# Fused attention and two expert layers on one core: the subtraction that makes the low halves of the exponentials, in pieces of 576 columns

## The chip, the cores and the metric

One NeuronCore of a Trainium2 chip runs the kernel. The metric is the device time of one execution in microseconds (us), smaller is better. The engines are named as in the profile: PE (TensorE, matrix products), DVE (VectorE), ACT (ScalarE), POOL (GpSimd) and SP (SyncE, which here only starts DMAs).

## What is computed

```python
q_pool = q.reshape(B, H, S // 2, 2, D).mean(axis=3)        # B=2, H=8, S=1152, D=64
scores = q_pool @ k.transpose(0, 1, 3, 2) / np.sqrt(D)
scores = scores - np.max(scores, axis=-1, keepdims=True)
attn = np.exp(scores)
attn = attn / (np.sum(attn, axis=-1, keepdims=True) + 1e-09)
x = attn @ v                                   # 1152 tokens of 512
# moe: every token goes to one of 8 experts (argmax of a cosine score), 512 -> 1024 -> 512, relu
# moe2: out = ((x @ w_a) * (x @ w_b)) @ w_out, inner width 1536
```

## The kernel before

The program has three stages: attention (to about 265 us of the profiled span), the experts (to about 460 us) and the last, dense layer. Attention works on 8 pairs of heads; a pair has 9 units of 128 pooled queries against 1152 keys, so there are 72 units, numbered j. The order of instructions on each engine is written out by hand: `att_step(i)` issues, for step i, the scores of unit i on PE (L374), the row maximum `nm` of unit i on DVE (L379), the exponential of unit i-1 on ACT into a tile `e` of 128x1152 (L384), and for unit i-2 the split of `e` into two half-precision parts. The first part `ehl[:, 0]` is a rounded copy, on ACT (L396); at one or two places in a pair ACT does only the first 768 columns and DVE the other 384 (L398, the CAST rows). The second part `ehl[:, 1]` is `e` minus the first part (`lo16`, L407), on POOL, for units 63 and 67 on DVE. Two units share one `ehl` tile; when both are filled, SP starts one DMA that transposes the four parts into `eT` (L413). PE multiplies `eT` with the values (L461) seven steps after the scores. One unit in each pair but the last (number 6 of 9), and the last three units of all, are transposed on PE instead and have no `lo16`.

Each engine takes its instructions strictly in this order. Beside them DVE and ACT prepare the next pair: `kT` and `qT` (L71, L75, L225, L226) and the two parts of the values, `vh` on ACT (L259) and `vl` on DVE (L262; two of 128x576 in a pair, which read `vs` and `vh` from SBUF). POOL also makes `qd` (L188, three in a pair).

For batch 0 the routing of the tokens (small DVE instructions in a chain) runs beside units 40 and later. Units 48 to 62 (`LO_PARTS`) already have their subtraction in four instructions of 288 columns; all others have one of 1152. The tiles `e` rotate through 3 buffers (L384 waits for the subtraction three units before), `ehl` and `eT` through 3 each.

Of the kernel before, what the change touches and what calls it, by code (L numbers as in the profile page):

```python
# [43 lines left out]
LO_PARTS = range(48, 63)  # L44
# [17 lines left out]
def fused(ctx, tc, q, k, v, emb, tau, w1, w2, wa, wb, wo, out):  # L62
# [337 lines left out]
    def lo16(j):  # L400
        if j not in two_of:
            return
        ehl = U[j]["ehl"]
        eng = nc.vector if j in LO_DVE else nc.gpsimd
        n = 288 if j in LO_PARTS else 1152
        for a in range(0, 1152, n):
            eng.tensor_tensor(out=ehl[:, 1, a:a + n], in0=U[j]["e"][:, a:a + n], in1=ehl[:, 0, a:a + n], op=ALU.subtract)  # L407

# [369 lines left out]
    def att_step(i):  # L778
# [19 lines left out]
        at(rowmax, i)  # L798
        turn("d")
        at(lo16, i - 2)  # L800
        turn("s")
        at(trans, i - 2)
# [555 lines left out]
```

## Time and profile before

| | us |
|---|---|
| three runs of the kernel | 695.67, 695.88, 692.66 (median 695.67) |
| the profiled execution | 693.38 |
| its span | 691.7 |
| PE busy | 618.1 |
| DVE busy | 493.5 |
| ACT busy | 373.6 |
| POOL busy | 322.3 |

The profiled execution took 1.7 us more than its span. In the rows, a time stands as start and duration in us from the start of the span; what stands in brackets is how long the engine had been idle and what ended that. "x2" means that two instructions are told in one row, from the start of the first to the end of the last. [...]

### The profile page before, as it was taken

What the parts mean: (1) busy time and instruction counts of PE and PEld (TensorE: products, weight loads), DVE (VectorE), ACT (ScalarE), POOL (GpSimd) and SP (SyncE); (2) the same over time, 40 slices, a digit from 0 to 9 for tenths busy, and PEclk for the clock granted to TensorE, in tenths of its full rate; (3) what the DMA queues carried; (4) which work ended last, traced back from release to release, by engine and by line L of the source; (5) the groups of instructions that cost most, each with busy time, mean ns of one, the idle gap of its engine ahead of it and who ended that gap; (6) DMA issues with size and microseconds to landing.
All of it is one profiled execution on the core that took longest, in us unless ns stands there. A gap on an engine that the chain in (4) does not pass through costs nothing.

```text
span 691.7 us, 13314 instructions
## 1 busy us (share of the span) xinstructions
PE 618.1 (89%) x5280; PEld 556.1 (80%) x5280; DVE 493.5 (71%) x796; ACT 373.6 (54%) x518; POOL 322.3 (47%) x271
## 2 busy tenths in 40 slices
PE   6688979889878788998989987969999999999996
PEld 5477767778767677998879877859999999999995
DVE  5978989887899977659947697974355575665523
ACT  3868886987665766456545675426243324233210
POOL 3958878785767941433424665673011212112100
PEclk9779999998988899999999998999999999999998
DMA  9979899998987789884898986454012213121012
GB/s 290 269 176 233 200 217 234 213 211 198 196 198 184 180 202 263 279 277 124 292 332 252 366 315 226 124 160 160 1 62 81 101 62 123 61 70 54 0 46 95
DMA packets 203075, 123.27 MB, mean 178 GB/s; under 512 B 149240, under 2 KB 174840, under 8 KB 203008
## 3 DMA queue, kind: packets, MB, share of 16 engines
q1 hardware_dynamic: 201536, 117.65, 62.3%
q0 software_dynamic: 1472, 4.72, 1.9%
q8 instruction: 43, 0.70, 0.4%
q14 instruction: 24, 0.20, 0.1%
HBM read 72.11 MB, written 13.67 MB: 124 GB/s over the span
## 4 chain that ended last, share of the span: by engine, by line
PE 49%; DVE 22%; ACT 4%; DMA 4%; issue 4%; POOL 1%; SPq 1%; DVEq 0%; ACTq 0%
PE ps_s L1165 21%; PE ps_s L890 4%; DVE nm L379 4%; PE ps_o L1187 4%; PE ps_m L1187 3%; PE ps_y L1187 3%; PE ps_o L461 2%; PE ps_s L374 2%; DVE vl L262 2%; DMA w2r<-in_moe_w_dram 2%; PE ps_m L933 2%; DMA eT<-ehl 2%; PE ps_y L933 1%; DVE cvt L1078 1%; DVE cvt L1079 1%
## 5 line engine op out<-in xcount | busy, mean ns | idle before, releaser
L407 POOL TENSOR_TENSOR ehl<-e,ehl 128x288 f16<-128x288 f32 (+1 forms) x99 | 152.3, 1557 | 63.7 <-issue 31.7
L75 POOL TENSOR_TENSOR wl<-cvt,wh 128x512 fp32r<-128x512 f32 x36 | 48.6, 1364 | 150.1 <-ACT wh L71 146.5
L75 POOL TENSOR_TENSOR w2l<-w2r,w2h 128x512 fp32r<-128x512 f32 x42 | 66.1, 1592 | 92.4 <-ACT w2h L71 46.9
L384 ACT ACTIVATE e<-ps_s,nm 128x1152 f32<-128x1152 f32 x72 | 87.8, 1220 | 37.2 <-DVE nm L379 25.1
L379 DVE TENSOR_REDUCE nm<-ps_s 128x1 f32<-128x1152 f32 x72 | 97.2, 1350 | 12.9 <-PE ps_s L374 12.7
L374 PE MATMUL ps_s<-kTh,qT 64*128 64x512 f32 (+2 forms) x480 | 98.2, 398 | 2.3 <-issue 1.2
L461 PEld LDWEIGHTS <-eT 128*128 128x128 f16 x1863 | 74.8, 102 | 16.6 <-issue 5.6
L461 PE MATMUL ps_o<-vh,eT 128*128 128x65 f16 (+1 forms) x1224 | 78.4, 203 | 10.3 <-DMA eT<-ehl 3.1
L374 PEld LDWEIGHTS ps_s<-kTh,qT 64*128 64x128 f32 x480 | 74.2, 206 | 8.5 <-issue 2.4
L461 PE MATMUL ps_o<-vl,eT 128*128 128x65 f16 (+1 forms) x612 | 73.2, 203 | 0.0
L1175 DVE TENSOR_TENSOR asb<-ps_s,asb 128x384 f32<-128x384 f32 x36 | 20.0, 554 | 69.1 <-PE ps_s L1165 69.1
L396 ACT ACTIVATE ehl<-e 128x1152 f16<-128x1152 f32 (+1 forms) x62 | 69.1, 1114 | 0.0
L71 ACT ACTIVATE abh<-asb 128x384 fp32r<-128x384 f32 x36 | 18.9, 525 | 84.3 <-DVE asb L1175 84.3
L374 PE MATMUL ps_s<-kTl,qT 64*128 64x512 f32 (+2 forms) x240 | 47.9, 367 | 1.5 <-DVE kTl L75 1.5
L1170 ACT ACTIVATE asb<-ps_s 128x384 f32<-128x384 f32 x36 | 17.7, 492 | 57.5 <-PE ps_s L1165 57.2
L374 PEld LDWEIGHTS ps_s<-kTl,qT 64*128 64x128 f32 x240 | 44.3, 209 | 2.1 <-DVE kTl L75 2.1
L75 DVE TENSOR_TENSOR w1l<-w1r,w1h 128x1024 fp32r<-128x1024 f32 x32 | 41.0, 1280 | 4.4 <-ACT w1h L71 3.6
L890 PE MATMUL ps_s<-xhi,w1l 128*128 128x256 f32 x128 | 38.0, 297 | 4.0 <-DVE w1l L75 4.0
L890 PE MATMUL ps_s<-xhi,w1h 128*128 128x256 f32 x128 | 38.4, 300 | 0.0
L75 DVE TENSOR_TENSOR abl<-asb,abh 128x384 fp32r<-128x384 f32 x36 | 20.7, 574 | 24.5 <-ACT abh L71 24.5
L890 PE MATMUL ps_s<-xlo,w1h 128*128 128x256 f32 x128 | 37.7, 294 | 0.0
L71 ACT ACTIVATE w1h<-w1r 128x1024 fp32r<-128x1024 f32 x32 | 34.0, 1063 | 0.0
(277 smaller groups left out, 1743.5 us busy)
## 6 DMA issues: line engine op xcount, KB each, us to landing
w1r<-in_moe_w_dram SPq DMA_DIRECT2D x32, 512.0 KB, 5.6
w2r<-in_moe_w_dram SPq DMA_DIRECT2D x32, 512.0 KB, 5.9
raw<-in_moe_w_a_dram SPq DMA_DIRECT2D x6, 1024.0 KB, 5.4
raw<-in_moe_w_b_dram SPq DMA_DIRECT2D x6, 1024.0 KB, 6.2
raw<-in_moe_w_out_dram SPq DMA_DIRECT2D x6, 1024.0 KB, 5.1
vs<-in_v_dram SPq DMA_DIRECT2D x8, 576.0 KB, 5.1
qs<-in_q_dram SPq DMA_DIRECT2D x16, 256.0 KB, 4.2
ks<-in_k_dram SPq DMA_DIRECT2D x7, 576.0 KB, 5.9
```

The source lines that it names most:

```text
L71: nc.scalar.activation(out=dst, in_=src, func=AF.Copy)
L75: (engine or nc.vector).tensor_tensor(out=dst, in0=src, in1=hi.bitcast(F32), op=ALU.subtract)
L374: nc.tensor.matmul(ps[:, c:c + n], qT[x][r:r + 64, o:o + 128], kT[y][r:r + 64, h, k0:k0 + n], start=i == 0, stop=i == len(ops) - 1)
L379: nc.vector.tensor_reduce(out=nm, in_=U[j]["ps"][:, 256:1408], axis=AX.X, op=ALU.max, negate=True)
L384: nc.scalar.activation(out=e, in_=U[j]["ps"][:, 256:1408], func=AF.Exp, bias=U[j]["nm"])
L396: nc.scalar.activation(out=ehl[:, 0, :c], in_=U[j]["e"][:, :c], func=AF.Copy)
L407: eng.tensor_tensor(out=ehl[:, 1, a:a + n], in0=U[j]["e"][:, a:a + n], in1=ehl[:, 0, a:a + n], op=ALU.subtract)
L461: nc.tensor.matmul(o, eT[:, 9 * x + n, :], v_[:, KEYS[n], :], start=(n == 0 and x == 0 and v_ is vh), stop=(n == 8 and x == 1))
L890: nc.tensor.matmul(p[:, 256 * j:256 * j + 256], a[:, kk, P * j:P * j + P], x[:, kk, :], start=(kk == 0 and x is xhi and a is w1h), stop=(k ...
L933: nc.tensor.matmul(y, a[:, j, P * t:P * t + P], w[:, j, :], start=(c == 0 and j == 0 and a is hh and w is w2h), stop=(c == 3 and j == 1 an ...
L1165: nc.tensor.matmul(p[:, :384], w[:, kk, :], y[:, kk, :], start=(kk == 0 and x == 0), stop=(kk == 3 and x == 2))
L1187: nc.tensor.matmul(F[n]["o"][t], a[:, P * t:P * t + P], w, start=(j == 0 and x == 0), stop=(j == 1 and x == 2))
```

## The change

```diff
         ehl = U[j]["ehl"]
         eng = nc.vector if j in LO_DVE else nc.gpsimd
-        n = 288 if j in LO_PARTS else 1152
+        n = 288 if j in LO_PARTS else 576
         for a in range(0, 1152, n):
             eng.tensor_tensor(out=ehl[:, 1, a:a + n], in0=U[j]["e"][:, a:a + n], in1=ehl[:, 0, a:a + n], op=ALU.subtract)
```

47 subtractions on POOL and 2 on DVE (units 63 and 67) become two instructions each. The same elements are read and written.

On POOL, in the third pair, the rows before (each row one instruction: its line, what it writes and reads, its size, and the engines and DMA queues whose semaphores it waits for):

```order
L407 TENSOR_TENSOR ehl<-e,ehl 128x1152 [waits Activation_49]
L188 TENSOR_TENSOR qd<-qs 128x384 [waits DMAHW1_49,DMAHW0_49]
L407 TENSOR_TENSOR ehl<-e,ehl 128x1152 [waits DMAHW2_49,Activation_49,Pool_49]
L407 TENSOR_TENSOR ehl<-e,ehl 128x1152 [waits DVE_49,Activation_49]
L407 TENSOR_TENSOR ehl<-e,ehl 128x1152 [waits DMAHW4_49,Activation_49,Pool_49]
L256 MEMSET vh 128x9 [waits PE_49]
```

And the same place now:

```order
L407 TENSOR_TENSOR ehl<-e,ehl 128x576 [waits Activation_49]
L407 TENSOR_TENSOR ehl<-e,ehl 128x576
L188 TENSOR_TENSOR qd<-qs 128x384 [waits DMAHW1_49,DMAHW0_49]
L407 TENSOR_TENSOR ehl<-e,ehl 128x576 [waits DMAHW2_49,Activation_49,Pool_49]
L407 TENSOR_TENSOR ehl<-e,ehl 128x576
L407 TENSOR_TENSOR ehl<-e,ehl 128x576 [waits Activation_49]
L407 TENSOR_TENSOR ehl<-e,ehl 128x576 [waits DVE_49]
L407 TENSOR_TENSOR ehl<-e,ehl 128x576 [waits DMAHW4_49,Activation_49,Pool_49]
L407 TENSOR_TENSOR ehl<-e,ehl 128x576
L256 MEMSET vh 128x9 [waits PE_49]
```

The second half of a unit waits for nothing, except in the units whose last 384 columns DVE has cast, where the wait for DVE has moved to the second half.

On ACT, in the fourth pair, before (e and ps_s are the exponentials and the scores):

```order
L384 ACTIVATE e<-ps_s_1531,nm 128x1152 [waits DVE_49,Pool_49]
L396 ACTIVATE ehl<-e 128x1152 [waits DMAHW0_49,Activation_49]
L71 ACTIVATE kTh<-ps_m 128x512 [waits PE_49]
L384 ACTIVATE e<-ps_s_1589,nm 128x1152 [waits DVE_49,Pool_49]
L396 ACTIVATE ehl<-e 128x1152 [waits Activation_49]
```

And now:

```order
L384 ACTIVATE e<-ps_s_1553,nm 128x1152 [waits DVE_49,Activation_49,Pool_49]
L396 ACTIVATE ehl<-e 128x1152 [waits DMAHW0_49,Activation_49]
L71 ACTIVATE kTh<-ps_m 128x512 [waits PE_49]
L384 ACTIVATE e<-ps_s_1611,nm 128x1152 [waits DVE_49,Pool_49]
L396 ACTIVATE ehl<-e 128x1152 [waits Activation_49]
```

36 of the 72 exponentials have a further wait, for ACT itself; the DMAs that transpose have a wait for ACT added in the same way. No instruction but the subtractions has another place in its row.

## Rows read from the trace of the kernel before

**Rows 1.** The page: span, and busy time of each engine.

```profile
span 691.7 us, 13314 instructions
PE 618.1 (89%) x5280; PEld 556.1 (80%) x5280; DVE 493.5 (71%) x796; ACT 373.6 (54%) x518; POOL 322.3 (47%) x271
```

**Rows 2.** Stretches: length, busy us (instructions) by engine, PEclk, DMA share, GB/s.

```profile
62.00:92.00 30.00, 26.39 (x403) 22.63 (x401) 27.40 (x49) 25.91 (x31) 24.30 (x14) 1.00 0.94 218
121.00:151.00 30.00, 26.95 (x406) 23.37 (x407) 27.57 (x50) 26.32 (x33) 23.68 (x14) 1.00 1.07 210
460.00:691.70 231.70, 225.54 (x1196) 210.88 (x1195) 119.37 (x177) 74.41 (x123) 42.60 (x35) 0.99 0.22 73
```

**Rows 3.** POOL's subtractions of 1152: busy us, mean ns, idle before them.

```profile
L407 POOL TENSOR_TENSOR ehl<-e,ehl 128x1152 f16<-128x1152 f32 x47 | 114.5, 2439 | 51.3 <-issue 22.1 <-ACT ehl L396 14.0 <-PE ps_m L204 11.6
```

**Rows 4.** Timeline of POOL: start us, duration us, instruction.

```profile
25.16 7.67 POOL L407 TENSOR_TENSOR ehl<-e,ehl 128x1152 f16<-128x1152 f32 x3
...
42.15 2.38 POOL L407 TENSOR_TENSOR ehl<-e,ehl 128x1152 f16<-128x1152 f32 x1 [6.47 <-PE ps_m L204]
...
76.42 5.22 POOL L407 TENSOR_TENSOR ehl<-e,ehl 128x1152 f16<-128x1152 f32 x2
...
85.87 2.38 POOL L407 TENSOR_TENSOR ehl<-e,ehl 128x1152 f16<-128x1152 f32 x1
...
188.64 2.81 POOL L407 TENSOR_TENSOR ehl<-e,ehl 128x288 f16<-128x288 f32 x4
```

**Rows 5.** Timeline of DVE: the values' second part, the casts, one subtraction.

```profile
29.29 4.17 DVE L262 SCALAR_TENSOR_TENSOR vl<-vs,vsc,vh 128x576 f16<-128x576 f32 x2
...
42.49 2.66 DVE L262 SCALAR_TENSOR_TENSOR vl<-vs,vsc,vh 128x576 f16<-128x576 f32 x1
...
51.05 1.45 DVE L262 SCALAR_TENSOR_TENSOR vl<-vs,vsc,vh 128x576 f16<-128x576 f32 x1
...
59.56 0.90 DVE L398 CAST ehl<-e 128x384 f16<-128x384 f32 x1
...
72.43 0.81 DVE L262 SCALAR_TENSOR_TENSOR vl<-vs,vsc,vh 128x576 f16<-128x576 f32 x1
...
77.81 1.59 DVE L262 SCALAR_TENSOR_TENSOR vl<-vs,vsc,vh 128x576 f16<-128x576 f32 x1
...
86.47 2.00 DVE L398 CAST ehl<-e 128x384 f16<-128x384 f32 x1
...
101.41 2.28 DVE L262 SCALAR_TENSOR_TENSOR vl<-vs,vsc,vh 128x576 f16<-128x576 f32 x1
...
171.27 2.38 DVE L262 SCALAR_TENSOR_TENSOR vl<-vs,vsc,vh 128x576 f16<-128x576 f32 x1
...
192.24 0.72 DVE L653 TENSOR_TENSOR oh<-L,rmx 128x40 f32<-128x40 f32 x1
...
245.80 1.35 DVE L407 TENSOR_TENSOR ehl<-e,ehl 128x1152 f16<-128x1152 f32 x1
...
255.54 0.35 DVE L398 CAST ehl<-e 128x384 f16<-128x384 f32 x1
```

**Rows 6.** Timeline at 234 us: POOL's twelve quarters, and DVE.

```profile
234.10 8.91 POOL L407 TENSOR_TENSOR ehl<-e,ehl 128x288 f16<-128x288 f32 x12
...
235.02 4.67 DVE L262 SCALAR_TENSOR_TENSOR vl<-vs,vsc,vh 128x576 f16<-128x576 f32 x1
```

**Rows 7.** PE after a stop: timeline, then the stretch behind it.

```profile
45.80 0.56 PE L424 MATMUL ps_m<-ident,e 128*128 128x128 f32 x3 [2.14 <-DVE kTl L75]
...
45.80:48.00 2.20, 2.20 (x32) 2.10 (x34) 1.80 (x3) 1.38 (x2) 2.20 (x2) 0.59 0.01 5
```

**Rows 8.** The chain of waits at a transposing DMA: start us, us, what.

```profile
143.63 10.69 DMA eT<-ehl
```

**Rows 9.** ACT's waits ahead of the exponentials: duration ns, min/median/max.

```profile
L384 ACTq EVENT_SEMAPHORE  x62: 17/17/38, 20.7 to 265.7; - x62
```

## Prediction

> **What bounds the kernel now.** I read the page first, then a table of stretches, then the timelines of POOL and DVE side by side, last the chain of waits. PE is busy for 618.1 of 691.7 us [rows 1], but that is an average: in the last 231.7 us it is busy for 225.5 with POOL at 42.6 [rows 2], and nothing that the change touches runs there. The edited instructions lie between 18 and 263 us, in attention. There no engine is full: in the stretches 62 to 92 and 121 to 151 us, which hold about one pair each, DVE is busy for 27.40 and 27.57 of 30.00 us, PE for 26.39 and 26.95, ACT for 25.91 and 26.32, POOL for 24.30 and 23.68, and the DMA share is 0.94 and 1.07 [rows 2]. DVE is the fullest, PE stands 0.6 to 1.0 us behind it. So a microsecond saved on DVE is not wholly a microsecond of the end.
>
> Part of DVE's busy time is waiting. `vl` alone takes 0.81 us (at 72.43), but 2.66 at 42.49, 2.28 at 101.41 and 2.38 at 171.27; the cast alone takes 0.35 (255.54), but 2.00 at 86.47 [rows 5]. In each case a subtraction of POOL was running: one ran from 42.15 for 2.38, to 44.53 [rows 4], and `vl` ended at 45.15, so that its own 0.81 began at 44.34, 0.19 before POOL's end. Either DVE starts about when POOL ends, or it doesn't wait at all. The small routing instructions behind quarters of 288 columns wait less: 0.72 at 192.24 [rows 5].
>
> **The change, part by part.**
>
> *What POOL pays.* Four quarters took 2.81 us where one piece takes 2.38 [rows 4]: three more starts cost 0.43, so one costs 0.14. Two halves then take 2.52, and the 47 units cost 6.6 us of POOL. Most of that lies in POOL's idle time, 51.3 us ahead of these instructions [rows 3]. The cover is gone where units stand one behind the other: the chain goes through a transposing DMA at 143.63, for 10.69 us [rows 8], which starts as soon as the fourth unit of such a run is done; 4 x 0.14 = 0.56 us later now. There is one more such run, a pair of pairs earlier. Between 0 and 1.1 us for both; I take 0.6, the middle, since half of the time PE has other work until the DMA lands.
>
> *What DVE gets.* If DVE comes in behind the first half, that is at 1.26 - 0.19 = 1.07 us after POOL's start in place of 2.38 - 0.19 = 2.19, it wins 1.12 us wherever it arrives within the first 1.07 us. At 42.49 it arrives 0.34 after POOL, at 86.47 0.60 after 85.87 [rows 4, 5]. There are six such places: `vl` at 42.49, 101.41 and 171.27, the second `vl` of the row at 29.29, behind the third of the units from 25.16, and two casts of 2.00, of which one stands in the rows. 6 x 1.12 = 6.7 us. At eight others DVE arrives in the second half, as at 77.81, which is 1.39 after 76.42 [rows 4, 5] and the earliest of them; they wait 0.14 longer, 1.1 us. Net 5.6 us less on DVE. By the table of stretches [rows 2] PE is late next, 0.6 to 1.0 us behind DVE in each pair, and ACT just behind it; with in-order queues less than that comes through. I take half, 2.8 us, and keep 0 and 5.6 as ends.
>
> [...]
>
> *What ACT pays.* 36 exponentials get a third wait, each an own entry in ACT's row. They are long fulfilled, and such an entry takes 17 ns [rows 9]: 0.6 us, half of it on the path, 0.3. The DMAs' added wait costs as little, and only the two on the chain count.
>
> *What DVE pays.* Units 63 and 67 have two starts. Two pieces of 576 columns are at most 2 x 0.81 = 1.62, against 1.35 in one [rows 5]: 0 to 0.27 each; I take 0.1 for both, since the 0.81 belongs to a heavier instruction.
>
> *Does the port come free between two halves?* This is the term on which the sign rests, and no row shows halves. For it: at 192.24 the small instruction waited about 0.5 us behind a quarter within a unit and then ran, as some twenty others of the routing do, and two casts; and between whole units DVE always got in, as at 77.81, in the middle of two units that stand back to back. Against it: at 235.02 `vl` took 4.67 us while POOL ran twelve quarters without a pause from 234.10 [rows 6]. Their pace is 0.69 us, so five or six of them went past the waiting `vl`. One loss among over twenty; I take it that DVE gets in. [...]
>
> *Sum.* -2.8 (DVE) - 1.0 (PE's clock) + 0.6 (transposes) + 0.3 (ACT) + 0.1 (DVE's starts) = -2.8 us. Against the profiled execution's 693.38 that gives 690.6. This execution lies 2.3 below the median of the runs shown, 695.67; on the median the forecast is 695.67 - 2.8 = **692.9 us**, 0.4% faster. A measurement of this kernel can tell about 0.5%, 3.5 us, from no change, so this counts as no change.
>
> **The rivals.**
>
> 1. *All of it comes through.* DVE sets the pace of attention, its 5.6 us are saved whole, and PE keeps its clock at the three places: -5.6 - 2.9 + 1.0 = -7.5, so 688.2. For it: DVE's 91% and `vl` on the chain; at 42.49 both the wait and PE's slow stretch lie ahead of the same next row maximum. Against it: PE and ACT within 1.7 us of DVE, and a DMA share about 1 [rows 2], which a shorter attention doesn't lighten.
>
> 2. *DVE doesn't come in, and nothing else happens.* Every one of the fourteen waits is 0.14 longer, 2.0 us, half of it on the path, 1.0; with the transposes' whole 1.1 and ACT's and DVE's 0.4 it is +2.5, so 698.2: no change either.
>
> 3. *DVE starves where units stand back to back.* As at 235.02 it also misses the gap between two units, which are now a row of halves, and waits for a whole further unit, 2.5 us. The places are the units from 25.16, those at 76.42 and the two that stand the same way a pair of pairs later: 3 x 2.5 = 7.5, half on the path 3.8, on top of rival 2: +6.3, so 702.0. It decides (more than 3.5 us slower) from the first such place on: 2.5 + 1.25 = 3.75. For it: the row at 235.02. Against it: these three places have whole pieces now, and DVE gets in at all three.
>
> That the change doesn't do what it says is excluded by the order of instructions; only DVE could be elsewhere, since every shift of 0.3 us moves an arrival from one half to the other (77.81 misses the first half by 0.32).
>
> **How the numbers follow.** The forecast with half of the gain 0.48, a quarter of that (0.12) beyond 3.5 us faster; rival 1 0.24; rival 2 0.12; rival 3 0.12; shifts that put POOL's lateness on more of the transposes 0.04. Faster 0.12 + 0.24 = 0.36, same 0.36 + 0.12 = 0.48, slower 0.12 + 0.04 = 0.16. The range: from rival 1, 688.2, with 0.7 for the scatter of the runs, 687.5, to a little over rival 2, 699.0, which leaves out most of rival 3 and the rest.
>
> **What would show it.** In the new profile no `vl` or cast before 182 us should be over 1.9 us (0.81 + 1.07), and the six places should be 1.0 to 1.1 shorter; POOL's L407 should be busy about 6 to 7 us more. If the three slow stretches of PE are gone and attention ends by 7 us earlier, rival 1 holds. If a `vl` of over 2.4 us stays, DVE doesn't get in between halves; if one is over 3, rival 3. If POOL's halves end later than 2.6 us after their start with no DVE instruction between them, a start costs more than 0.14. The forecast is wrong if the DMA waits of PE grow by more than 3 us, or if the stretch behind 265 us, which I take as shifted whole, changes its length.

## The result, and the profile after

The changed kernel takes 684.14 us (median of 20 runs, 678.55 to 687.96), the kernel before 691.98 in as many runs beside it (687.15 to 695.88). The ratio is 0.9897, 95% interval 0.9875 to 0.9919: **about 7.1 us or 1.0% faster**. The forecast was 692.9 with a range from 687.5, and no change as the likeliest case, so it was wrong: the time lies below its range. Two things are in the miss of 8.8 us. 3.7 of it is the base: I put the sum on the median of three runs, 695.67, and over 20 runs the kernel before takes 691.98 (from that base the range would have begun at 683.8). The rest, 4 to 5 us, is the sum itself: -2.8 in place of -7.1. One execution of the experiments, of the kernel without the conflict and in halves, ran in a slower state of the chip, and its ratio and median leave it out.

The page of the changed kernel, span and busy time of each engine (to be set beside [rows 1]):

```profile
span 683.4 us, 13368 instructions
PE 612.4 (90%) x5280; PEld 550.5 (81%) x5280; DVE 484.0 (71%) x798; ACT 373.2 (55%) x518; POOL 328.4 (48%) x318
```

DVE has lost 9.5 us, POOL has gained 6.1. POOL's subtractions in halves in the changed kernel, grouped by shape (busy us, mean ns, idle before them), where [rows 3] had 47 of 1152 columns in 114.5 us:

```profile
L407 POOL TENSOR_TENSOR ehl<-e,ehl 128x576 f16<-128x576 f32 x94 | 124.6, 1349 | 35.6 <-issue 25.7 <-ACT ehl L396 8.5 <-POOL qd L188 0.9
```

The timeline of POOL in the changed kernel (start us, duration us), the same places as in [rows 4]:

```profile
25.71 8.52 POOL L407 TENSOR_TENSOR ehl<-e,ehl 128x576 f16<-128x576 f32 x6
...
41.80 3.04 POOL L407 TENSOR_TENSOR ehl<-e,ehl 128x576 f16<-128x576 f32 x2 [5.02 <-issue]
...
52.23 2.52 POOL L407 TENSOR_TENSOR ehl<-e,ehl 128x576 f16<-128x576 f32 x2
...
225.73 8.95 POOL L407 TENSOR_TENSOR ehl<-e,ehl 128x288 f16<-128x288 f32 x12
```

And the timeline of DVE in the changed kernel, which answers to [rows 5] and, with its last three rows, to [rows 6] and what follows there:

```profile
29.60 3.49 DVE L262 SCALAR_TENSOR_TENSOR vl<-vs,vsc,vh 128x576 f16<-128x576 f32 x2
...
41.88 1.82 DVE L262 SCALAR_TENSOR_TENSOR vl<-vs,vsc,vh 128x576 f16<-128x576 f32 x1
48.11 0.81 DVE L262 SCALAR_TENSOR_TENSOR vl<-vs,vsc,vh 128x576 f16<-128x576 f32 x1
...
86.13 0.92 DVE L398 CAST ehl<-e 128x384 f16<-128x384 f32 x1
100.17 1.05 DVE L262 SCALAR_TENSOR_TENSOR vl<-vs,vsc,vh 128x576 f16<-128x576 f32 x1
105.63 0.81 DVE L262 SCALAR_TENSOR_TENSOR vl<-vs,vsc,vh 128x576 f16<-128x576 f32 x1
...
192.79 1.35 DVE L262 SCALAR_TENSOR_TENSOR vl<-vs,vsc,vh 128x576 f16<-128x576 f32 x1
...
226.63 3.31 DVE L262 SCALAR_TENSOR_TENSOR vl<-vs,vsc,vh 128x576 f16<-128x576 f32 x1
234.35 1.61 DVE L407 TENSOR_TENSOR ehl<-e,ehl 128x576 f16<-128x576 f32 x2
235.88 0.81 DVE L262 SCALAR_TENSOR_TENSOR vl<-vs,vsc,vh 128x576 f16<-128x576 f32 x1
```

At 41.88 `vl` arrives 0.08 after POOL's start and ends at 43.70, so its own 0.81 began at 42.89, 1.09 after POOL's start: behind the first half. In turn the second half came later: the three pairs of halves with a `vl` in between took 3.04, 3.05 and 3.04 (from 41.80, 99.32 and 165.70), an undisturbed one 2.52. No `vl` or cast ahead of 182 us is over 1.83 now; before, the longest took 2.92 (the second `vl` of the row at 29.29) and 2.66.

How far each place has moved shows where the gain is made. The `vl` at 200.30, the first for the pair of heads numbered 6, is at 192.79 (-7.5). The `vl` at 235.02 is at 226.63 (-8.4), and its successor has come from 247.06 to 235.88 (-11.2). Of these further 2.8 us, 1.4 are the shorter wait of this `vl` (3.31 in place of 4.67), beside subtractions that the change leaves as they were; where the other 1.4 come from isn't separated. The first expert matmul (L890) has come from 271.1 to 261.7 (-9.4) and the end of the span from 691.7 to 683.4 (-8.3). So nearly all is made in the first 190 us; some more at 226 to 236, and most of that is given back behind it.

What is waited for there stands in the chain of waits. In the changed kernel, from 246 us (start, duration, what the chain went through):

```profile
249.87 2.53 POOL ehl L407 x2
252.40 4.32 SPq L413
...
256.89 4.64 SPq L413
...
263.50 5.54 DMA xr<-xbuf
269.04 0.14 issue
269.18 0.63 PE ps_t L838 x4
```

The same stretch in the kernel before goes through DVE:

```profile
235.10 4.58 DVE vl L262
...
245.80 1.35 DVE ehl L407
247.15 0.73 DVE vl L262
...
257.87 1.80 DVE ehl L407
```

Once DVE is early, the chain goes through POOL's last subtractions, the transposes behind them in SP's queue, and the read of `xr`, the tokens of the second group of expert matmuls, that is queued behind those; PE stands still for it for 2.02 us ahead of 269.18.

### The profile page after: what moved, and what is told of

Its sections match the earlier page's. It is cut to its first block, busy times and chain, and to the rows that moved or that the text cites. A ratio compares the mean times of both kernels' runs of the same rounds, so it can differ in the third digit from the quotient of the medians.

```text
span 683.4 us, 13368 instructions
## 1 busy us (share of the span) xinstructions
PE 612.4 (90%) x5280; PEld 550.5 (81%) x5280; DVE 484.0 (71%) x798; ACT 373.2 (55%) x518; POOL 328.4 (48%) x318
## 3 DMA queue, kind: packets, MB, share of 16 engines
q0 software_dynamic: 1472, 4.72, 2.0%
## 4 chain that ended last, share of the span: by engine, by line
PE 43%; DVE 7%; DMA 4%; issue 3%; SPq 3%; POOL 2%; ACT 1%; DVEq 0%; ACTq 0%
PE ps_s L1165 21%; PE ps_s L890 4%; PE ps_o L1187 4%; PE ps_m L1187 4%; PE ps_y L1187 4%; DMA w2r<-in_moe_w_dram 2%; PE ps_m L933 1%; PE ps_o L933 1%; PE ps_y L933 1%; SPq L413 1%; DVE cvt L1079 1%; PE ps_s L895 1%; DVE cvt L1078 1%; DVE w1l L75 1%; DMA ybuf<-ys 1%
## 5 line engine op out<-in xcount | busy, mean ns | idle before, releaser
L407 POOL TENSOR_TENSOR ehl<-e,ehl 128x576 f16<-128x576 f32 (+1 forms) x146 | 162.0, 1137 | 45.5 <-issue 34.3
L384 ACT ACTIVATE e<-ps_s,nm 128x1152 f32<-128x1152 f32 x72 | 87.9, 1221 | 35.5 <-DVE nm L379 23.4
L374 PE MATMUL ps_s<-kTh,qT 64*128 64x512 f32 (+2 forms) x480 | 95.0, 387 | 2.4 <-issue 1.3
L461 PEld LDWEIGHTS <-eT 128*128 128x128 f16 x1863 | 72.9, 100 | 21.0 <-DMA eT<-ehl 15.0
L461 PE MATMUL ps_o<-vh,eT 128*128 128x65 f16 (+1 forms) x1224 | 76.7, 201 | 14.6 <-DMA eT<-ehl 12.3
L374 PEld LDWEIGHTS ps_s<-kTh,qT 64*128 64x128 f32 x480 | 71.2, 198 | 8.7 <-issue 2.9
L461 PE MATMUL ps_o<-vl,eT 128*128 128x65 f16 (+1 forms) x612 | 71.7, 201 | 0.0
L374 PE MATMUL ps_s<-kTl,qT 64*128 64x512 f32 (+2 forms) x240 | 46.0, 353 | 0.7 <-DVE kTl L75 0.7
L374 PEld LDWEIGHTS ps_s<-kTl,qT 64*128 64x128 f32 x240 | 42.4, 201 | 1.3 <-DVE kTl L75 1.3
L890 PE MATMUL ps_s<-xhi,w1l 128*128 128x256 f32 x128 | 38.1, 297 | 4.0 <-DVE w1l L75 4.0
L890 PE MATMUL ps_s<-xhi,w1h 128*128 128x256 f32 x128 | 38.3, 300 | 0.0
L890 PE MATMUL ps_s<-xlo,w1h 128*128 128x256 f32 x128 | 37.7, 294 | 0.0
```

The lines of the kernel that those rows point to most:

```text
L374: nc.tensor.matmul(ps[:, c:c + n], qT[x][r:r + 64, o:o + 128], kT[y][r:r + 64, h, k0:k0 + n], start=i == 0, stop=i == len(ops) - 1)
L384: nc.scalar.activation(out=e, in_=U[j]["ps"][:, 256:1408], func=AF.Exp, bias=U[j]["nm"])
L461: nc.tensor.matmul(o, eT[:, 9 * x + n, :], v_[:, KEYS[n], :], start=(n == 0 and x == 0 and v_ is vh), stop=(n == 8 and x == 1))
L890: nc.tensor.matmul(p[:, 256 * j:256 * j + 256], a[:, kk, P * j:P * j + P], x[:, kk, :], start=(kk == 0 and x is xhi and a is w1h), stop=(k ...
```

## The experiments

The ratios are against the kernel before on the same chip, the diffs against its code. The line that most of them change is L405, in `lo16`.

**Without the conflict, whole and in halves.** Two kernels without the DVE instructions that took longer beside POOL ahead of the routing, `vl` (0.81 to 2.92 us before) and the casts (0.90 to 2.00): the casts go wholly to ACT, and `vl` is set to zero by a memset, which leaves the second part of the values out of the result. The first keeps whole subtractions:

```diff
-HI_ACT = (1152, 1152, 1152, 1152, 1152, 768, 1152, 1152, 768)
+HI_ACT = (1152,) * 9
-HI_ACT2, HI2 = (1152, 1152, 1152, 1152, 1152, 1152, 768, 1152, 768), (48, 70)
+HI_ACT2, HI2 = (1152,) * 9, (48, 70)
-            nc.vector.scalar_tensor_tensor(out=D["vl"][:, :, 65 * h:65 * h + 64], in0=vs[:, h], scalar=vsc,
-                                           in1=D["vh"][:, :, 65 * h:65 * h + 64], op0=ALU.mult, op1=ALU.subtract)
+            nc.vector.memset(D["vl"][:, :, 65 * h:65 * h + 64], 0.0)
```

> The kernel before, whole pieces of 1152, with the DVE instructions that read two operands from SBUF or copy from SBUF in attention taken out: vl is set to zero by a memset (so the values' low part is left out of the result) and ACT rounds all 1152 columns of every unit (no casts on DVE). Theory P (DVE waits for the port that POOL holds, and these waits set the pace of attention): faster than before by more than the change itself brought, 1.5 to 2.5% (about 17 us of DVE waiting and work less, ACT 8 x 0.35 = 3 us more). Rival R (the gain comes from elsewhere: smaller pieces hand over earlier, or the waits of POOL, ACT and SP are arranged otherwise): 0 to 1% faster, by the work that is left out.

The second has the change as well:

```diff
-        n = 288 if j in LO_PARTS else 1152
+        n = 288 if j in LO_PARTS else 576
```

> The same as e1_no_conflict_whole, with halves of 576 outside the routing. The low part of the values is left out here too. Theory P: nothing is left to win, and POOL's 47 further starts of 0.14 us remain: the same as e1 or up to 0.4% slower. Rival R: 0.8 to 1.2% faster than e1, as the change was.

Measured: 0.9815 [0.9760, 0.9870] whole, 0.9781 [0.9730, 0.9833] in halves; medians 678.62 and 678.87. The timeline of DVE in the whole one:

```profile
39.46 0.54 DVE L262 MEMSET vl<- 128x576 f16 x1
```

and in the one with halves:

```profile
40.89 0.54 DVE L262 MEMSET vl<- 128x576 f16 x1
```

In both the memset takes 0.54 with a subtraction of POOL beside it, which in the whole one ran from 39.36 for 2.38. The first lies in the 1.5 to 2.5% that the conflict as cause had asked for. The ratios favour halves by 0.35%, the medians lie within 0.04%, and in the profiled executions the `vl` of pair 6 comes at 186.43 whole and 192.01 in halves. Without `vl` and the casts, these two single executions show nothing of the 7.5 us that the change wins up to that place. The intervals alone would still allow a gain of 1%, so this is a hint, not a proof; that DVE's time is what counts is shown by the stretches under "More DVE work", below.

**Which units make the gain.** Halves only in units 0 to 47:

```diff
-        n = 288 if j in LO_PARTS else 1152
+        n = 288 if j in LO_PARTS else 576 if j < 48 else 1152
```

> Halves only for units 0 to 47; units 63 to 68 keep one piece of 1152, on POOL and on DVE. Theory P: the gain is made ahead of the routing, by 185 us: 0.9 to 1.2% faster than before, as the change or a little better (0.2 to 0.5 us of DVE's starts at 234 and 247 us saved). Rival L (a good part of the gain is made behind the routing, where the profile shows attention 2.8 us shorter between 235 and 255 us): 0.5 to 0.7% faster.

Measured: 0.9889 [0.9835, 0.9943], as much as the change. The interval alone would allow up to half of the gain to lie behind unit 47, but the `vl` of pair 6 (191.19) and the first expert matmul (260.40) stand no later than in the changed kernel (192.79 and 261.67): of a gain by the units from 63 on nothing is seen.

**More DVE work.** The change, and in five of the pairs two further reductions of `vs` on DVE, which nobody reads:

```diff
+                if i >= 2 and 1 <= pr <= 5:
+                    more = small.tile([P, 1], F32, name="more")
+                    nc.vector.tensor_reduce(out=more, in_=D["vs"].rearrange("p h t d -> p (h t) d"), axis=AX.XY, op=ALU.max)
-        n = 288 if j in LO_PARTS else 1152
+        n = 288 if j in LO_PARTS else 576
```

> The change, with one more row maximum of the values' tile on DVE (1.27 us, one SBUF operand, no wait for POOL) behind each vl of pairs 1 to 5, where vl waited for POOL before: ten instructions, 12.7 us of DVE; their result is not used. It measures how much of DVE's time in this place reaches the end. Theory D (DVE sets the pace of attention whole): 12 to 13 us, 1.7 to 1.9% slower than the change. Half, as the prediction took: 6.4 us, 0.9%. Rival (DVE off the path): under 0.3%.

Measured: 1.0155 [1.0107, 1.0204]; against the change's 0.9897 that is 2.6% or 18 us more. One row of DVE's timeline and, below it, the `vl` of pair 6 and the late one:

```profile
43.52 1.34 DVE L301 TENSOR_REDUCE more<-vs 128x1 f32<-128x1152 f32 x1
...
205.55 1.36 DVE L262 SCALAR_TENSOR_TENSOR vl<-vs,vsc,vh 128x576 f16<-128x576 f32 x1
...
240.32 7.06 DVE L262 SCALAR_TENSOR_TENSOR vl<-vs,vsc,vh 128x576 f16<-128x576 f32 x1
```

The next instruction starts 1.27 after such a reduction, so the ten cost DVE 12.7 us. The `vl` of pair 6 comes at 205.55 in place of 192.79: 12.76 later. **A microsecond more of DVE is a microsecond there**, not half of one. Of the other 5 us, 3.3 come through the late `vl`: it takes 7.06 in place of 3.31, and the first expert matmul stands 38.37 behind its start in place of 35.04.

The stretch from the `vl` at about 42 us to the first `vl` of pair 6 (length; PE, PEld, DVE, ACT, POOL busy; PE's granted clock as a share of full speed, DMA share, GB/s) tells more of this factor. In order: before, the change, more DVE work; without the conflict whole and in halves; quarters (below).

```profile
42.49:200.30 157.81, 137.41 (x1907) 119.39 (x1903) 138.41 (x256) 126.01 (x156) 119.91 (x81) 0.95 0.97 208
41.88:192.79 150.91, 132.72 (x1907) 115.33 (x1903) 132.23 (x257) 125.46 (x156) 125.19 (x118) 0.98 1.06 219
42.26:205.55 163.29, 137.69 (x1907) 119.18 (x1903) 144.76 (x267) 126.36 (x155) 124.81 (x118) 0.95 1.08 205
39.46:186.43 146.97, 130.40 (x1903) 113.58 (x1903) 122.84 (x251) 126.63 (x156) 114.90 (x82) 0.99 1.12 228
40.89:192.01 151.12, 136.82 (x1903) 119.56 (x1903) 124.34 (x251) 127.36 (x155) 120.95 (x120) 0.93 1.09 226
42.24:205.84 163.60, 139.86 (x1907) 122.04 (x1903) 136.86 (x256) 125.32 (x155) 134.78 (x192) 0.92 1.00 212
```

A wait for POOL counts as busy here, as in the 2.66 of the `vl` at 42.49 before. The length less DVE's busy time is 19.4 us before, 18.7 with the change and 18.5 with more work: DVE's idle time stays, and the stretch follows its busy time one for one. Without the conflict it grows to 24.1 and 26.8, so there DVE no longer sets the pace alone: with halves, 7.9 us less of DVE than with the change make the stretch no shorter (151.12 and 150.91, at a clock of 0.93 and 0.98).

**Thirds.**

```diff
-        n = 288 if j in LO_PARTS else 1152
+        n = 288 if j in LO_PARTS else 384
```

> Three pieces of 384 outside the routing. Theory P: a wait that begins at a random point in a unit is 0.6 us with halves and 0.4 with thirds, over about 16 waits 2 to 3 us less on DVE, against 47 x 0.14 = 6.6 us more on POOL, which now runs at 0.83 of the stretches ahead of the routing and feeds the transposing DMAs that PE already waits for: within 0.3% of the change. Rival R2 (the number of starts on POOL costs nothing as long as DVE waits less): 0.3 to 0.5% faster than the change.

Measured: 0.9892 [0.9857, 0.9927], the same as halves. The exponentials' wait for POOL grows, but the `vl` of pair 6 is none the later for it (192.01). In this kernel, L384 by line (busy, mean ns, idle and what ended it):

```profile
L384 ACT ACTIVATE e<-ps_s,nm 128x1152 f32<-128x1152 f32 x72 | 87.9, 1221 | 39.0 <-DVE nm L379 17.7 <-POOL ehl L407 12.8 <-DVE pos L726 3.4
```

and in the changed kernel:

```profile
L384 ACT ACTIVATE e<-ps_s,nm 128x1152 f32<-128x1152 f32 x72 | 87.9, 1221 | 35.5 <-DVE nm L379 23.4 <-POOL ehl L407 4.3 <-DVE pos L726 3.4
```

**Quarters up to unit 56, whole pieces behind it.**

```diff
-        n = 288 if j in LO_PARTS else 1152
+        n = 288 if j < 57 else 1152
```

> Quarters of 288 for units 0 to 56 and one piece for units 57 to 68. Theory P: waits of DVE ahead of the routing fall to 0.35 us each at random, 3 to 4 us less than with halves, while POOL runs 38 x 0.28 = 11 us longer there and nears its whole time (0.9 of the stretches); the transposing DMAs start later. The same as halves with late whole pieces, or up to 0.4% slower. Rival R2 (POOL's starts cost nothing): 0.3 to 0.5% faster than halves with late whole pieces.

Measured: 1.0066 [1.0035, 1.0097], slower than before. Its rows for L407, L384 and `vl` by line:

```profile
L407 POOL TENSOR_TENSOR ehl<-e,ehl 128x288 f16<-128x288 f32 x204 | 149.1, 763 | 39.3 <-issue 35.7 <-ACT ehl L396 3.3 <-DVE ehl L398 0.3
L384 ACT ACTIVATE e<-ps_s,nm 128x1152 f32<-128x1152 f32 x72 | 87.9, 1221 | 43.8 <-DVE nm L379 17.5 <-POOL ehl L407 14.4 <-DVE pos L726 3.4
...
L262 DVE SCALAR_TENSOR_TENSOR vl<-vs,vsc,vh 128x576 f16<-128x576 f32 x16 | 15.5, 974 | 0.0
```

`vl` waits least of all here (974 ns, 1354 in the changed kernel), and yet the `vl` of pair 6 comes at 205.84, 13.05 later. By the stretches, DVE is busy for 4.6 us more than with the change and idle for 8.1 more. The first is because other instructions of DVE are passed over, in POOL's longer unbroken runs: two casts take 3.23 and 2.16 (0.92 and 0.82 with the change), and two of the routing's (0.18 and 0.70 with the change) take 2.61 and 2.87, the first beside the four quarters that POOL ran from 189.42 to 192.21:

```profile
189.66 2.61 DVE L558 TENSOR_TENSOR L<-L 128x40 f32<-128x40 f32 x1
192.19 2.87 DVE L561 TENSOR_SCALAR rn<-rn 128x5 f32<-128x5 f32 x1
```

For the second it is likely, but not shown, that POOL has become late: it is busy for 9.6 us more in this stretch. The exponentials' wait of 14.4 us for it doesn't tell, since with thirds it is 12.8 and nothing is lost there. My expectation was too small; the whole pieces behind unit 56 have a part in the end too, which this run doesn't separate, but the 13 us stand ahead of them.

**Halves everywhere**, also in units 48 to 62:

```diff
-        n = 288 if j in LO_PARTS else 1152
+        n = 576
```

> Halves of 576 for all units, beside the routing too (units 48 to 62 had quarters). Theory P: each of some twenty small routing instructions on DVE waits about 0.25 us longer behind a half than behind a quarter, which is +5 us at most, against 13 x 0.28 = 3.6 us less on POOL; and the run of twelve quarters, past which vl waited for 3.31 us in the profile of the change, becomes six halves. Within 0.5% of the change; slower by up to 0.7% if the routing's chain takes the waits whole.

Measured: 0.9962 [0.9932, 0.9992], 0.65% slower than the change. The second `vl` of pair 6 comes at 204.66 (202.42 with the change), the next at 235.39 (226.63). The routing's small DVE instructions beside these units do better with quarters: from the first `vl` of pair 6 to that next one DVE is busy for 5.4 us more, and two of them (L616, L620) take 2.86 and 2.32 in place of 0.20 and 0.15.

**Whole pieces in units 57 to 62**, to take the long wait at 226.63 away:

```diff
-        n = 288 if j in LO_PARTS else 1152
+        n = 288 if 48 <= j < 57 else 1152 if 57 <= j < 63 else 576
```

> The change, with units 57 to 62 in one piece of 1152 in place of four quarters. In the profiles the vl instruction that meets the run of twelve quarters took 4.67 us (before), 3.31 (the change), 0.98 (halves for units 0 to 47 only) and 7.99 (thirds). Theory S (without a pause between pieces POOL's next piece often passes the waiting DVE instruction, so its wait is a matter of chance there): with whole units vl takes between 0.81 and 3.0 us in that place, every time, and the kernel is 0.2 to 0.6% faster than the change. Rival (the long vl there is hidden): the same as the change within 0.1%.

Measured: 0.9919 [0.9879, 0.9959], not faster than the change. DVE's timeline:

```profile
217.20 2.30 DVE L398 CAST ehl<-e 128x384 f16<-128x384 f32 x1
...
221.06 3.09 DVE L625 CAST pyi<-ok 128x5 int32<-128x5 f32 x1
...
232.81 2.96 DVE L262 SCALAR_TENSOR_TENSOR vl<-vs,vsc,vh 128x576 f16<-128x576 f32 x1
```

Units 57 and 58 hold DVE up (2.30 and 3.09; 0.67 and 0.17 with the change), and `vl` arrives 6.2 later than with the change.

**The late run alone.** Units 59, 61 and 62 follow each other on POOL without a pause, right behind the DMAs that scatter the tokens. Three kernels change the pieces of this run: whole (units 59 on), halves in 59 to 62 and whole behind, and whole with the casts on ACT.

```diff
-        n = 288 if j in LO_PARTS else 1152
+        n = 288 if 48 <= j < 59 else 1152 if j >= 59 else 576
```

> The change, but of the quarters only units 48 to 58 keep them (those that run beside the routing's last instructions); units 59, 61 and 62, whose twelve quarters stand in one unbroken row at 226 to 235 us, and units 63 to 68 are in one piece of 1152. So the two whole units that held DVE at 217 and 221 us in e7_halves_late_whole (2.30 and 3.09 us) are quarters again. Theory S (without a pause the next piece passes the waiting vl by chance): vl in that place takes 0.8 to 2.4 us in place of 0.98, 3.31, 4.67, 7.06 or 7.99, and the kernel is 0.2 to 0.5% faster than the change, ratio to before 0.985 to 0.988. Rival (what vl loses there is hidden): ratio 0.989 to 0.990.

```diff
-        n = 288 if j in LO_PARTS else 1152
+        n = 288 if 48 <= j < 59 else 1152 if j >= 63 else 576
```

> As e10_late_run_whole, but units 59, 61 and 62 in halves: a row of six pieces. If DVE gets in behind the first half, vl takes about 1.2 us and this is 1 us faster than e10; by theory S it sometimes is passed by later halves and takes up to 6 us. The same as e10 within 0.3%; a vl of over 2.4 us in its profile would show that halves can pass too.

```diff
-HI_ACT = (1152, 1152, 1152, 1152, 1152, 768, 1152, 1152, 768)
+HI_ACT = (1152,) * 9
-HI_ACT2, HI2 = (1152, 1152, 1152, 1152, 1152, 1152, 768, 1152, 768), (48, 70)
+HI_ACT2, HI2 = (1152,) * 9, (48, 70)
-        n = 288 if j in LO_PARTS else 1152
+        n = 288 if 48 <= j < 59 else 1152 if j >= 59 else 576
```

> As e10_late_run_whole, and ACT rounds all 1152 columns of every unit, so that DVE makes no casts. Theory D (DVE's time in attention reaches the end whole): eight casts, 6.3 us of DVE in the profile of the change, go, and ACT works 8 x 0.35 = 2.8 us longer; 0.3 to 0.7% faster than e10. Rival (ACT, at 24 to 28 of 30 us, is the next to bind): the same as e10 or up to 0.3% slower.

Measured: 0.9897 [0.9867, 0.9928], 0.9909 [0.9875, 0.9942] and 0.9884 [0.9854, 0.9914]: none can be told from the change. The last was to be 0.3 to 0.7% faster than the first if DVE's time reached the end whole, and the same if ACT bound next; 0.13% tells neither. Up to the `vl` of pair 6, which comes at 190.18 in place of 192.27, DVE is busy for 2.9 us less without the casts. In the kernel with halves `vl` takes 4.72, so it is passed over by halves too. POOL's run in the kernel with whole pieces:

```profile
226.10 7.59 POOL L407 TENSOR_TENSOR ehl<-e,ehl 128x1152 f16<-128x1152 f32 x3
```

and `vl` on DVE beside it:

```profile
227.00 4.46 DVE L262 SCALAR_TENSOR_TENSOR vl<-vs,vsc,vh 128x576 f16<-128x576 f32 x1
```

`vl` ends at 231.46, so it began its 0.81 at 230.65, 4.55 after POOL's start and hence behind the second whole piece (two of 2.38 end at 4.76, less 0.19 as in the prediction): it missed the gap behind the first. So it is not only small pieces that make it miss. All executions with this run side by side (us; the last column is the first expert matmul less the start of `vl`):

| kernel | pieces in the run | `vl` behind POOL's start | `vl` takes | first L890 | from `vl` to L890 |
|---|---|---|---|---|---|
| halves in 0 to 47 | 288 | 1.85 | 0.98 | 260.40 | 35.07 |
| the change | 288 | 0.90 | 3.31 | 261.67 | 35.04 |
| whole, no casts | 1152 | 1.99 | 3.37 | 260.82 | 34.91 |
| late run whole | 1152 | 0.90 | 4.46 | 262.53 | 35.53 |
| before | 288 | 0.92 | 4.67 | 271.06 | 36.04 |
| late run in halves | 576 | 0.91 | 4.72 | 261.44 | 35.75 |
| more DVE work | 288 | 1.86 | 7.06 | 278.69 | 38.37 |
| thirds | 288 | 0.92 | 7.99 | 265.79 | 39.95 |

Two things are to be seen. Neither the pieces nor the arrival tell how long `vl` waits. And up to about 3.4 us it costs nothing: 35 us is what the rest needs anyhow; in the changed kernel PE waits in it for two transposing DMAs, 2.76 us at 250.07 and 0.71 at 258.83. Beyond that the end of attention moves with it, by 3.3 us for 7.06 and 4.9 for 7.99.

## Why the prediction was wrong, point by point

**POOL's price was right.** Two halves take 2.52 undisturbed, as worked out; POOL is busy for 6.1 us more, forecast 6.6. DVE's own starts were dearer than I took: its two units take 1.61 and 2.01 in place of 1.35 and 1.80, 0.47 us together, forecast 0.1.

**DVE gets in between halves: right**, at each place ahead of the routing. At the first it began 1.09 behind POOL's start, forecast 1.07. A missed gap would have left `vl` at 2.3 to 3.1 at three of these places (2.52 - 0.19, less the arrival, + 0.81); it took 1.82, 1.05 and 1.16. In the late run it did miss gaps (3.31, and 4.67 before), and so did instructions with quarters (2.61 at 189.66) and with halves everywhere (2.86 and 2.32). (Missed gaps between halves alone would have been the second rival; the third also needs missed gaps between whole units.) The port of which the prediction and theory P speak no run shows: the traces show when DVE's instructions begin and end, not what the two engines share.

**What DVE saves was a little small.** The six places save 6.1 us (0.84 and 1.23 and 1.22 on `vl`, 0.68 on the two in one row, 1.08 on each cast; forecast 6.7). The others were to lose 1.1 and won 1.1: with everything earlier some arrivals no longer meet POOL, as the second `vl` of the pair, 1.45 at 51.05 [rows 5] and 0.81 at 48.11 now. Together -7.2, forecast -5.6.

**The step that failed is "I take half, 2.8 us".** I read from the busy shares in [rows 2] that PE and ACT stand a microsecond behind DVE and would be late next. The stretches of the changed kernel (length; PE, PEld, DVE, ACT, POOL busy; granted clock, DMA share), for the three pairs that began at 42.40, 72.40 and 101.40 before and then lasted 30.0, 29.0 and 29.6 us:

```profile
41.80:69.60 27.80, 23.72 (x351) 20.25 (x348) 24.93 (x44) 23.75 (x28) 24.17 (x21) 1.00 0.97 200
69.60:100.10 30.50, 27.16 (x396) 23.52 (x394) 25.29 (x48) 24.87 (x32) 25.37 (x23) 0.94 1.12 226
100.10:126.90 26.80, 23.29 (x339) 19.82 (x336) 24.20 (x45) 23.35 (x27) 23.38 (x21) 1.00 1.12 230
```

Three pairs take 85.1 in place of 88.6 us. The busy time of PE and ACT was no second wall: PE's longest waits in attention were for what DVE hadn't yet made (`kTl` 10.4 us, `qT` 8.3), and with DVE early they closed up. DVE's 7.2 us came through whole (7.5 at the `vl` of pair 6), the run with 12.7 us more on DVE, 12.76 later, says the same from the other side, and DVE's idle time over these pairs is 19.4, 18.7 and 18.5 us in the three kernels. A factor of 1 in place of a half gives -5.6 - 1.0 + 1.0 = -5.6 by my own terms, and with the 7.2 measured -7.2. That this meets the 7.1 so closely is in part luck, since the other terms in it are not confirmed one by one.

**PE's clock can't be separated.** No run shows the 1.0 us that the sum has for PE's clock, nor the 2.9 of rival 1. What the traces show is that the stop came down from 2.14 us [rows 7] to 1.30, and the next 2.2 us are at 1.00 in place of 0.59. PE in the changed kernel:

```profile
44.36 0.55 PE L424 MATMUL ps_m<-ident,e 128*128 128x128 f32 x3 [1.30 <-DVE kTl L75]
```

```profile
44.30:46.50 2.20, 2.14 (x39) 2.08 (x39) 2.13 (x6) 1.34 (x3) 2.20 (x3) 1.00 0.61 209
```

The three slow stretches are gone, as I had asked as a sign of rival 1: the pairs from 42, 101 and 165 us had 0.94, 0.94 and 0.95 before and have 1.00 now. But the second pair has fallen from 1.00 to 0.94 and is 1.5 us longer. Over all five the clock is 0.98 in place of 0.95, and DVE's idle time, in which a faster PE would show beside all else, is 0.7 us less. Four experiments have the change's code up to 182 us, and their `vl` of pair 6 stands at 191.19 to 192.45, against 192.79: executions of one code differ by 1.6 us there, more than this 0.7 or the 1.0 that I gave to the clock.

**The transposes were undersized.** I had written that PE's waits for DMAs growing by more than 3 us would speak against the forecast. They grew by 9.2, from 3.1 in 4 to (changed kernel: us in total, times, longest):

```profile
PE ps_o L461 <- DMA eT<-ehl: 12.3, 11, 2.8
...
PE ps_m L424 <- DVE kTl L75: 7.2, 5, 3.0
```

while the waits for `kTl` fell from 10.4 to 7.2. So something does come late next, the transposing DMAs and not PE; but the seven waits ahead of 190 us (6.3 us together) don't keep the `vl` of pair 6 from coming 7.5 earlier. Where a cost can be seen is the end of attention, where 1.8 us of what the late `vl` had won are lost (-11.2 to -9.4).

**ACT's third wait and the stretch behind 265.** ACT is busy for 373.2 us, 373.6 before; 0.3 us can't be seen. From the first expert matmul to the end of the span are 421.7 us, 420.6 before, and 418.6 to 422.5 in the experiments, so this stretch is shifted whole as far as single executions can tell.

**The rivals.** Rival 1, 7.5 us faster, is what happened in size: on 691.98 it gives 684.5. Its reason, that DVE sets the pace and all of it comes through, holds; that its number does too is partly luck, with 5.6 for DVE where 7.2 were saved, and 2.9 for the clock, which is not shown. Rival 2 falls with the rows of DVE ahead of 182 us. Rival 3 falls where it was placed: behind the units from 25.71 the row of two `vl` takes 3.49, 0.68 less than before.

## What to carry over

Here DVE's wait lasted about as long as POOL's instruction, and cutting that in two took the wait at the first `vl` from 1.85 us to 1.01 (2.66 and 1.82, less its own 0.81) for the price of one start, 0.14 us of POOL. What such a cut brings is told by whether the waiting engine sets the pace; DVE's busy share of 0.91 with PE at 0.88 didn't say "half of it", since PE's longest waits in attention were for DVE (18.7 us for `kTl` and `qT`). Its idle time said more: in three kernels it stayed (19.4, 18.7 and 18.5 us) while the stretch changed with its busy time. Work added on that engine tells the factor in one run, but only for more of it: without the conflict DVE's idle time grew to 24.1 and 26.8, so the factor of one ends somewhere. And more pieces brought no more: thirds 0.9892, the same as halves, and with quarters ahead of the routing `vl` takes least (974 ns in the mean), casts and routing longer (up to 3.23 and 2.87), and the kernel is slower than before (1.0066).

## What was not expected of the hardware

In the unbroken run of three units behind the scatter DMAs `vl` took 0.98 to 7.99 us (its own 0.81 included), though POOL goes from one instruction to the next every 0.7 to 2.5 us there, and in the changed kernel `vl` and the casts got in at the next such change everywhere ahead of 182 us. Pieces of 288, 576 and 1152 and the moment of arrival don't explain it. Nor does it need this run: a cast at 148.60 took 3.23 us between quarters, where no scatter stands beside it, and two instructions of the routing took 2.86 and 2.32 beside halves (under "Halves everywhere"). What decides is open.

Not every DVE instruction waits for POOL. In the run with more DVE work the ten reductions of `vs`, which read one tile from SBUF, took 1339 to 1349 ns, the one at 43.52 beside the second half of a unit, which POOL ended at 44.74 there, and the memsets at 39.46 and 40.89 in the two kernels without the conflict took 0.54. `vl`, with two tiles from SBUF, took up to 2.92 before and up to 1.83 with the change ahead of 182 us, where 0.81 is its own, and the casts up to 2.00 and 1.20, where 0.35 is theirs. And DVE can be passed over by several instructions in a row: the routing instruction at 189.66 in the kernel with quarters arrived 0.24 behind the start of the first of four quarters and ended at 192.27, 0.06 behind the end of the last.
